# Transposes first in VectorE's turn, mirror loads ahead of the check's, and a second late Q product: one reordering of a Fourier and linear attention kernel

## The chip, the cores and the metric

The kernel runs on one core of a Trainium2 chip. Its engines are TensorE (PE in the profile; its weight loads are PEld), VectorE (DVE), ScalarE (ACT), GpSimd (POOL) and SyncE (SP), which here does nothing but issue DMA transfers. The metric is the time of one execution on the device in microseconds (us), the median of several runs.

## The reference

Two rounds of two blocks on x of 2048 rows and 640 columns, in float32:

```python
x = x + fourier(layernorm(x), dft_seq, dft_hid)
x = x + attention(layernorm(x), wqkv, wo)
x = x + fourier(layernorm(x), dft_seq, dft_hid)
x = x + attention(layernorm(x), wqkv, wo)

def fourier(x, re, im):                  # real part of a 2-D DFT
    a, b = x @ hid_re.T, x @ hid_im.T
    return seq_re @ a - seq_im @ b

def attention(x, wqkv, wo):              # 32 heads of 20 columns
    q, k, v = heads(x @ wqkv)
    pq, pk = phi(q), phi(k)              # t + 1 for t > 0, else exp(t); + 1e-6
    kv, z = pk.T @ v, pk.sum(rows)
    return rows((pq @ kv) / (pq @ z + 1e-6)) @ wo
```

The Fourier matrices are inputs. The kernel uses their symmetries, and checks on the chip that the inputs have them; that check is a part of what VectorE does.

## The kernel before

**Tiles.** The 2048 rows are 16 tiles of 128 rows by 640 columns. A float32 product is made from three products of rounded halves: each operand is split into a hi part (a cast on ScalarE, L125) and a lo part (a subtraction, L126, on VectorE or GpSimd), and hi x hi, hi x lo and lo x hi are added. So one tile's product with a 640 x 640 weight is 30 matrix products of 320 columns (L177).

**A turn.** The attention block's `keys_values` (L282 on) runs two loops, over tiles 0 to 9 and 10 to 15 (`CUT` is 10). Turn n makes K of tile n (30 products), phi of it (three passes on ScalarE, L302 to L304, and one on VectorE, L305), adds it to the sum of K over the rows on GpSimd (L325), and makes Q of tile n and its phi. K and Q need tile n normalized, transposed, and split in hi and lo, and that was made in turn n-1. After each loop `gram` multiplies the tiles with their phi(K), which gives, once V's weight is applied in `combine`, what the reference calls kv. `total` (L390) adds five products with the sum of K.

**Two ways to transpose.** Tiles 1 to 3 are transposed on TensorE (L131). For tiles 4 to 15 (`TURNED`) the normalized tile (L119) is stored to memory (`turn_out`, L139), loaded again in another arrangement (`turn_in`, L144, the "mirror" load), and transposed in 32 x 32 blocks by VectorE (`turned`, L149). `LEADS` (3, 2): turn n normalizes and stores tile n+3, loads tile n+2, and transposes and splits tile n+1.

**The check.** `Check` holds pieces of the Fourier matrices to be compared. `fetch` (L1099) loads up to four tiles of some 346 KB (`ck`), `step` (L1107 to L1124) compares them on VectorE: one reduction, then five custom two-input operations. `STEPS` says after which turns and grams a step is given out; before the change a step ends with the fetch of the next. `SAVES` says when parts of the weights are stored for layer 1, two stores of 320 KB each.

**Order.** SP issues its transfers in the order in which the program is written. The instructions of the other engines are placed by a scheduler, which follows the order of writing unless the table `AHEAD` gives a piece of work an earlier or later place; a step's own operations stay in order among themselves. A late query (`keep`, 1 in both layers) is a Q product that is not made in its turn but at the start of `combine`, where it covers work on other engines. In `combine` the kv products (L432) are followed by a mask (VectorE and GpSimd, from L442) and a hi and lo split, before products with the output weight, 120 rows at a time.

Of the kernel before, what the change touches and what calls it, by code (L numbers as in the profile page):

```python
# [30 lines left out]
STEPS = ((1, 2, 4, 5, 6, 7, 10, 11, 12), (1, 6, 8, 9, 12))  # L31
SAVES = ((4, 5, 8, 13, 15), (1, 4, 8, 10, 11))
# [16 lines left out]
AHEAD = {'2keep00': -60, '2out10': -600, '1q13': 60, '2keep01': 600, '2keep02': 5, '2out02': -20, '1q14': 60, '2out01': 20, '0m1': 60, '0kv5': 200, '1weigh15': -20, '1res13': 5, '2out12': -200, '2weigh1': 5, '2first': 60, '2out13': -200, '0lo10': -200, '0lo03': -600, '0lo02': 20, '0key1': -60, '0key10': 200, '0stats6': -5, '0w0': 200, '0lo13': -60, '0out02': 600, '0pks8': -5, '0stats2': 600, '0hi11': 200, '0lo11': 60, '0normed3': 600, '0out00': -600, '0out11': 5, '0chunks3': 5, '0pks0': 200, '0keep10': 60, '0keep02': 20, '0out03': 600, '0key4': -60, '0chunks4': 20, '0lo12': -60, '0chunks7': -5, '0gram7': -600, '0gram6': -200, '0chunks5': -60, '0chunks13': 60, '0wo0': -20, '0chunks15': -5, '0normed0': -60, '0gram15': 200, '0norm2': 200, '0query15': 5, '0pks2': -60, '0wo5': 5, '0gram2': 200, '0gram8': 5, '0normed4': 5, '0key12': -5, '0stats3': -20, '0stats0': -600, '0query6': 200, '0norm12': 200, '0gram9': -20, '0gram1': 60, '0norm15': -20, '0chunks8': 200, '0weigh1': 60, '0stats8': -200, '0hi00': -5, '0hi13': 5, '0m2': 200, '0query13': 600, '0norm8': -60, '0norm13': 600, '0gram13': -60, '0norm5': -200, '0gram5': -60, '0pks9': -60, '0norm11': -200, '0stats1': 20, '0keep00': 600, '0gram10': -200, '0normed8': 600, '0pks5': 5, '0m5': 20, '0norm7': -600, '0key6': 600, '0query1': 20, '0query2': -60, '0stats7': 60, '0norm0': -5, '0key14': 5, '0weigh0': 20, '0m0': -600, '0query14': -60, '0normed9': 60, '0key8': -5, '0pks10': -600, '0chunks0': 600, '0pz0': -200, '0query12': -5, '0stats12': 20, '0query4': 600, '0zb': -600, '0stats5': 20, '0query10': 200, '2hi12': -600, '3res10': -200, '2pz6': 60, '2norm14': 200, '2kv5': -5, '2pks1': 60, '2hi02': 600, '3q13': -5, '2weigh13': 600, '2norm5': 5, '3q11': 600, '2stats1': -60, '3q5': -200, '2key3': -20, '3weigh11': -20, '2pz4': -20, '3weigh1': -600, '3res9': -20, '2begin': -20, '2hi00': -600, '2stats6': -200, '2stats7': 5, '2chunks1': -20, '2norm2': -600, '3q7': -600, '2kv3': -200, '3res2': 200, '2wo4': -5, '2query6': -600, '2normed8': -600, '2pks0': 20, '2normed6': -60, '2lo02': -60, '2key9': -20, '2chunks9': 20, '2keep10': -20, '2gram11': 200, '2weigh11': -60, '2chunks2': 60, '2pz0': -60, '2m2': -200, '2stats14': 600, '3res13': 600, '2stats10': 200, '3q2': 600, '2key10': 60, '0kv3': -60, '0wo4': 5, '0stats4': 60, '0wo3': -200, '0norm4': -5, '0wo2': -20, '0query7': -600, '0pks1': 200, '0norm10': 60, '0key5': -60, '0normed6': -60, '0pks11': 200, '0pks3': 200, '0pks7': 200, '0normed1': 20, '0chunks9': -20, '0normed13': 20, '0chunks6': 600, '0out12': -60, '0norm1': -20, '0m3': -5, '0stats10': -20, '0normed7': -5, '0key11': 200, '0key9': 60, '0begin': 600, '0lo01': 600, '0gram4': 5, '0query3': -200, '0normed15': -60, '0hi10': -200, '0kv1': 5, '0key0': -200, '0key7': -5, '0chunks2': -60, '0out13': -200, '0chunks11': -600, '0norm6': 5, '0stats14': 60, '0pks14': 20, '0kv0': -200, '0stats13': 5}  # L49


class K:
# [59 lines left out]
    def norm(self, x, out, stats):  # L112
        m, rs, act = stats
        if act == "neg":
            self.nc.vector.tensor_scalar(out, x, m, rs, op0=ALU.add, op1=ALU.mult)
        elif act:
            self.nc.scalar.activation(out, x, AF.Identity, bias=m, scale=rs)
        else:
            self.nc.vector.tensor_scalar(out, x, m, rs, op0=ALU.subtract, op1=ALU.mult)  # L119
# [22 lines left out]
    def turn_in(self, src):  # L142
        z = self.temp()
        self.nc.sync.dma_start(z, src.rearrange("a (j t) c -> (a j) (t c)", t=4))  # L144
        return z

    def turned(self, z, pool):
        t = self.temp()
# [3 lines left out]
        return self.split_chunks(t, pool)  # L152

    def split_chunks(self, tp, pool=0):
        hi, lo = self.temp(F32R), self.temp(F32R)
        self.split(tp[:, :D], hi, lo, pool)
# [25 lines left out]
class Attention:  # L182
    def __init__(self, k, X, order, order2, wqkv, wo, mask, saved=None):
# [3 lines left out]
        self.turns, self.tlows = (TURNED[k.layer], TLOWS[k.layer]) if saved is not None else ((), ())  # L187
# [35 lines left out]
    def normed(self, n):  # L223
# [6 lines left out]
        with self.k.ahead("norm", n):  # L230
            if n in self.turns:
                self.k.norm(x, xn, self.kept[n])
# [841 lines left out]
class Check:  # L1074
# [28 lines left out]
    def step(self, more):  # L1103
# [25 lines left out]
        if more:  # L1129
            self.fetch()  # L1130
# [292 lines left out]
```

## Time and profile before

| | |
|---|---|
| median of 3 runs | 770.46 us (768.66 to 771.43) |
| the profiled execution's own time | 769.41 us |
| its span in the profile | 767.6 us, granted clock 0.997 in the mean |
| PE busy | 736.0 us (96%) |
| VectorE busy | 628.5 us (82%) |
| ScalarE, GpSimd busy | 341.8 us (45%), 261.7 us (34%) |
| DMA | 94.88 MB, mean 124 GB/s |

Where the work lies, in us from the start of the span: the first Fourier block to about 78, layer 0's turns with a first loop that ends at 174, its grams to 219, the second loop to 268, grams to 297, the combine to 315, outputs and the second Fourier block to about 446, layer 1's turns to 539, grams to 583, the second loop to 635, grams to 663, the combine to 682, and the outputs to the end.

An engine's busy time says little about what bounds the kernel where stages differ. The view of waits lists, for an engine, who it waited for, how long in total, how often and the longest; the view by windows gives busy time, granted clock and DMA share of each stretch; the chain of waits goes back from the last instruction and names at each step what was waited for. In all of them a name such as `t<-x,kept` says which tiles are written and read.

### The profile page before, as it was taken

How to read it: one execution, taken by the hardware profiler on the slowest of the kernel's cores; microseconds unless marked ns; L12 is line 12 of the kernel's file. 1: busy time of each engine (PE TensorE's matmuls, PEld its weight loads, DVE VectorE, ACT ScalarE, POOL GpSimd, SP SyncE). 2: the span in 40 equal slices, each digit the busy share in tenths (PEclk: the TensorE clock that was granted, in tenths of full speed). 3: DMA queues.
4: the chain of work that ended last, by engine and by line, in shares of the span. 5: the costliest groups of instructions: out<-in, count | busy, mean ns of one | idle time of the engine just before them, and what ended most of it. 6: DMA issues, size and time to landing. Idle time of an engine off the chain costs nothing.

```text
span 767.6 us, 12773 instructions
## 1 busy us (share of the span) xinstructions
PE 736.0 (96%) x4764; PEld 694.4 (90%) x4764; DVE 628.5 (82%) x1176; ACT 341.8 (45%) x642; POOL 261.7 (34%) x267
## 2 busy tenths in 40 slices
PE   4999999989999999999999999999999999999997
PEld 1388999989999999899977999999999899989996
DVE  7998988978689795988974897899868977599982
ACT  8745445454334553455682334545433445331110
POOL 5248922241012211467762694222101211243300
PEclk9999999999999999999999999999999999999999
DMA  9322346873276741400052223477316615001112
GB/s 332 100 76 89 107 149 190 258 235 110 65 250 201 246 146 26 154 3 2 11 195 70 69 100 118 147 217 234 87 43 215 189 46 151 22 12 68 71 70 73
DMA packets 51231, 94.88 MB, mean 124 GB/s; under 512 B 5044, under 2 KB 19127, under 8 KB 51159
## 3 DMA queue, kind: packets, MB, share of 16 engines
q1 hardware_dynamic: 51159, 93.96, 38.9%
q8 instruction: 40, 0.66, 0.4%
q14 instruction: 32, 0.26, 0.1%
HBM read 73.87 MB, written 19.66 MB: 122 GB/s over the span
## 4 chain that ended last, share of the span: by engine, by line
PE 51%; DVE 28%; ACT 8%; issue 6%; POOL 3%; DMA 3%; SPq 0%; DVEq 0%; POOLq 0%; ACTq 0%
PE ps L177 24%; PE ps L270 16%; DVE junk L1124 6%; PE ps L1049 4%; PE ps L995 3%; DVE t L126 3%; DVE t L149 2%; DVE t L119 2%; DVE w L126 2%; ACT t L125 2%; PE ps L131 1%; PE ps L954 1%; DVE pq L305 1%; DMA ck<-in_ck 1%; DVE st L99 1%
## 5 line engine op out<-in xcount | busy, mean ns | idle before, releaser
L177 PE MATMUL ps<-w,t 128*128 128x320 f32 x2880 | 438.9, 311 | 8.8 <-ACT t L125 5.8
L177 PEld LDWEIGHTS ps<-w,t 128*128 128x128 f32 x2880 | 424.1, 189 | 14.5 <-ACT t L125 10.1
L325 POOL TENSOR_TENSOR t<-t,s 128x640 f32<-128x640 f32 x32 | 64.6, 2018 | 284.7 <-DVE s L305 284.7
L270 PE MATMUL ps<-t,t 128*128 128x256 f32 (+1 forms) x640 | 139.9, 309 | 0.0
L270 PEld LDWEIGHTS ps<-t,t 128*128 128x128 f32 x640 | 106.8, 188 | 0.0
L1124 DVE CUSTOM_DVE_ANT_0 junk<-ck,ck 128x688 bf16<-128x688 f32 (+5 forms) x138 | 99.1, 718 | 4.7 <-DMA ck<-in_ck 1.8
L302 ACT ACTIVATE t<-ps 128x640 f32<-128x640 f32 x64 | 45.1, 705 | 125.1 <-PE ps L177 119.5
L270 PE MATMUL ps<-w,t 128*128 128x384 f32 (+1 forms) x320 | 98.9, 311 | 0.6 <-DVE w L126 0.6
L478 POOL TENSOR_TENSOR t<-pq,t 128x640 f32<-128x640 f32 x32 | 53.3, 1672 | 96.3 <-ACT t L401 46.6
L126 DVE TENSOR_TENSOR t<-t,t 128x640 fp32r<-128x640 f32 x56 | 50.2, 896 | 26.9 <-PE ps L270 16.1
L125 ACT CAST t<-t 128x640 fp32r<-128x640 f32 x56 | 40.8, 728 | 53.6 <-DVE t L119 26.5
L125 ACT CAST t<-ps 128x640 fp32r<-128x640 f32 (+1 forms) x42 | 28.9, 691 | 78.9 <-PE ps L131 77.9
L119 DVE TENSOR_SCALAR t<-x,kept 128x640 f32<-128x640 f32 x60 | 62.7, 1050 | 0.6 <-DMA turn<-t 0.6
L270 PEld LDWEIGHTS ps<-w,t 128*128 128x128 f32 x320 | 60.2, 188 | 1.6 <-DVE w L126 1.5
L995 PE MATMUL ps<-t,u 128*128 128x322 f32 x306 | 48.5, 316 | 1.4 <-ACT t L1022 0.7
L995 PEld LDWEIGHTS ps<-t,u 128*128 128x128 f32 x306 | 46.0, 190 | 2.8 <-ACT t L1022 0.9
L304 ACT ACTIVATE t<-t 128x640 f32<-128x640 f32 x64 | 47.4, 741 | 0.0
L126 DVE TENSOR_TENSOR t<-ps,t 128x640 fp32r<-128x640 f32 (+1 forms) x42 | 34.1, 815 | 5.8 <-ACT t L125 4.8
L305 DVE SCALAR_TENSOR_TENSOR pq<-t,pq 128x640 f32<-128x640 f32 x32 | 27.2, 852 | 13.3 <-ACT t L304 13.3
L149 DVE STREAM_TRANSPOSE t<-t 128x640 f32<-128x640 f32 x24 | 32.1, 1339 | 6.0 <-DMA t<-turn 6.0
L1049 PE MATMUL ps<-cw,ab 128*128 128x512 f32 x80 | 35.4, 596 | 1.6 <-ACT ab L819 0.9
L125 ACT CAST t<-s 128x640 fp32r<-128x640 f32 x32 | 23.2, 725 | 29.4 <-PE ps L270 29.4
(181 smaller groups left out, 905.7 us busy)
## 6 DMA issues: line engine op xcount, KB each, us to landing
ck<-in_ck SPq DMA_DIRECT2D x48, 346.0 KB
ck<-in_ck SPq DMA_DIRECT2D x48, 344.0 KB
turn<-t SPq DMA_DIRECT2D x24, 320.0 KB
t<-turn SPq DMA_DIRECT2D x24, 320.0 KB
save<-w SPq DMA_DIRECT2D x20, 320.0 KB
w<-save SPq DMA_DIRECT2D x20, 320.0 KB
x<-in_x SPq DMA_DIRECT2D x16, 320.0 KB
out<-x SPq DMA_DIRECT2D x15, 320.0 KB
```

Source lines behind the costliest of these rows:

```text
L119: self.nc.vector.tensor_scalar(out, x, m, rs, op0=ALU.subtract, op1=ALU.mult)
L125: self.nc.scalar.copy(hi, src)
L126: self.engine(pool).tensor_tensor(lo, src, hi.bitcast(F32), op=ALU.subtract)
L149: self.nc.vector.transpose(t.rearrange("p (b j t) -> p t b j", b=ND, t=4), z.rearrange("p (t b i) -> p t b i", t=4, b=ND))
L177: nc.tensor.matmul(pu[:m, 512 * h : 512 * h + HD], s, w[:, HD * h : HD * h + HD], start=first, stop=last)
L270: nc.tensor.matmul(self.place(G, c, part), x[:, 128 * c : 128 * c + 128], p[:, f : f + n], start=start and i == 0, stop=stop and i == 2, s ...
L304: nc.scalar.activation(e, e, AF.Exp, scale=-1.0)
L325: nc.gpsimd.tensor_tensor(pksum, pksum, pk, op=ALU.add)
L478: k.nc.gpsimd.tensor_tensor(t1, self.PQ[self.order2[n]], self.zb, op=ALU.mult)
L995: self.k.nc.tensor.matmul(po[:, o : o + 322], s[:, f : f + 128], w[:, x, :], start=start, stop=stop)
L1049: self.k.nc.tensor.matmul(self.sum(j), T.out["o", q][:, 128 * j : 128 * j + 128], self.C[2, g], start=n == 0, stop=n == 3)
L1124: i = nc.vector.tensor_tensor_reduce(k.junk[:, : a.shape[1]], b, a, 1.0, 0.0, op0, op1, o)
```

## The change

1. **Order of a turn.** For a turned tile, the parts of turn n are now written in the order `tfkq`: transpose and split of tile n+1 first, then the feed (norm and store of tile n+3, mirror load of n+2, and the check's fetch), then K, then Q. Before it was feed, K, transpose, Q. Other tiles keep the old order.
2. **The check.** `step` no longer fetches; the fetch stands behind the mirror load in the feed, and in the gram loop. Steps and saves move to other turns (`STEPS`, `SAVES`).
3. **Who does what.** Tile 7 of layer 1 is transposed on TensorE. In layer 0 the lo parts of tiles 7 and 15 are made on GpSimd (`TLOWS`; tile 3 is named too, but is not a turned tile). The norms of tile 2 in layer 0 and of 3 and 5 in layer 1 go to ScalarE (`ANORM`), statistics of more tiles too (`ASTATS`). Eight of the sums of K go from GpSimd to VectorE (`PKSUMS`). Mirror loads of tiles up to 13 take their buffer from Q's pool (`EARLY`).
4. **Late queries.** Layer 0 keeps two (`KEEP`): the first stays at the head of `combine`, the second comes after the kv products. The products of `total` come after the gram of tile 14 in layer 0 and 12 in layer 1, not 10 (`TOTAL`).
5. **Priorities.** Entries of `AHEAD` are changed, removed and added.

```diff
-STEPS = ((1, 2, 4, 5, 6, 7, 10, 11, 12), (1, 6, 8, 9, 12))
-SAVES = ((4, 5, 8, 13, 15), (1, 4, 8, 10, 11))
+STEPS = ((1, 2, 3, 4, 5, 6, 10, 11, 12), (2, 4, 8, 9, 12))
+SAVES = ((4, 5, 8, 10, 13), (0, 6, 7, 11, 12))
...
-TURNED = (tuple(range(4, 16)), tuple(range(4, 16)))
-TLOWS = ((), ())
+TURNED = ((4, 5, 6, 7, 8, 9, 10, 11, 12, 13, 14, 15), (4, 5, 6, 8, 9, 10, 11, 12, 13, 14, 15))
+TLOWS = ((3, 7, 15), ())
 LEADS = (3, 2)
+ORDERS = ('tfkq', 'tfkq')
+ANORM = ((2,), (3, 5))
+KEEP = (2, 1)
+TOTAL = (4, 2)
+EARLY = (14, 13)
+PKSUMS = ((1, 7, 13, 14), (2, 6, 11, 12))
...
-ASTATS = ((11,), (1,))
-VSTATS = ((4, 6, 8, 9, 10, 11, 13), ())
+ASTATS = ((4, 10, 11, 13, 14), (1, 4, 10, 15))
+VSTATS = ((0, 3, 4, 7, 8, 11, 13, 15), (1, 11, 13, 15))
...
-    def norm(self, x, out, stats):
+    def norm(self, x, out, stats, on_act=False):
         m, rs, act = stats
-        if act == "neg":
+        if on_act:
+            nb = self.small([128, 1], "nb")
+            self.nc.gpsimd.tensor_tensor(nb, m, rs, op=ALU.mult)
+            if act != "neg":
+                self.nc.gpsimd.tensor_scalar(nb, nb, -1.0, None, op0=ALU.mult)
+            self.nc.scalar.activation(out, x, AF.Identity, bias=nb, scale=rs)
+        elif act == "neg":
...
+                turns = n + 1 in self.turns
+                for what in ORDERS[k.layer] if turns else "fkcq":
+                    if what == "f":
+                        feed()
+                        if check is not None and check.more:
+                            check.fetch()
+                    elif what == "t":
+                        turn()
+                    elif what == "k":
+                        key()
+                        pks.append(pk)
+                    elif what == "c":
+                        if n and n + 1 < NT:
+                            chunks()
+                    elif n < NT - keep:
+                        query(mid=chunks if not turns and n + 1 < NT and not n else None)
+                    else:
+                        late.append(query)
...
+                if check is not None and check.more:
+                    check.fetch()
                 self.gram(G + [tail], ready, n == a, n == b - 1, a == 0)
...
-                if n == CUT:
+                if n == CUT + TOTAL[k.layer]:
                     self.total(G, pksum)
...
-        self.now = None
-        if more:
-            self.fetch()
+        self.now, self.more = None, more
```

VectorE in turn 4 of layer 0, before. `t_1377` is the transposed tile 5, L305 are phi of K (`s`) and of Q (`pq`), L119 the norm of tile 8, and L1107 and L1124 the check step (`ca`, `junk`, `cm`; the short read of the result after each piece is left out here and below).

```order
L149 STREAM_TRANSPOSE t_1377<-t_1242 128x4x160
L305 SCALAR_TENSOR_TENSOR s_1339<-t_1371,s_1339 128x640
L126 TENSOR_TENSOR t_1380<-t_1377,t_1379 128x640
L119 TENSOR_SCALAR t_1436<-x_96,kept_1437 128x640
L305 SCALAR_TENSOR_TENSOR pq_1383<-t_1415,pq_1383 128x640
L1107 TENSOR_REDUCE ca<-ck_1222 128x1
L1124 ISA junk,cm<-ck_1224,ck_1222 128x692
L1124 ISA junk,cm<-ck_1226,ck_1224 128x692
L1124 ISA junk,cm<-ck_1228,ck_1226 128x692
L1124 ISA junk,cm<-ck_1222,ck_1228 128x519
L1124 ISA junk,cm<-ck_1222,ck_1228 128x173
L149 STREAM_TRANSPOSE t_1488<-t_1337 128x4x160
```

And with the change (L161 is the transpose, L138 the lo part, L131 the norm, L321 phi, L1140 and L1157 the step):

```order
L161 STREAM_TRANSPOSE t_1333<-z_1242 128x4x160
L1157 ISA junk,cm<-ck_1125,ck_1131 128x173
L321 SCALAR_TENSOR_TENSOR pq_1289<-t_1321,pq_1289 128x640
L1140 TENSOR_REDUCE ca<-ck_1244 128x1
L1157 ISA junk,cm<-ck_1246,ck_1244 128x692
L138 TENSOR_TENSOR t_1335<-t_1333,t_1334 128x640
L131 TENSOR_SCALAR t_1339<-x_128,kept_1340 128x640
L1157 ISA junk,cm<-ck_1248,ck_1246 128x692
L1157 ISA junk,cm<-ck_1250,ck_1248 128x692
L321 SCALAR_TENSOR_TENSOR s_1332<-t_1392,s_1332 128x640
L1157 ISA junk,cm<-ck_1244,ck_1250 128x519
L161 STREAM_TRANSPOSE t_1444<-z_1351 128x4x160
```

The transpose moved ahead of the phi of the query of the turn before, the lo part and the norm now stand ahead of phi of K, and the step is spread through the turn instead of standing in one piece between phi of Q and the next transpose.

SP's queue around the same turns, before (`ck` are the check's tiles, `turn` the stores, `t` the mirror loads, `save` the weights' stores):

```order
L1099 DMA ck_1222<-in_ck 128x692
...
L1099 DMA ck_1228<-in_ck 128x692
L139 DMA turn_1240<-t_1230 128x4x160
L144 DMA t_1242<-turn_1127 128x640
L139 DMA turn_1335<-t_1325 128x4x160
L144 DMA t_1337<-turn_1240 128x640
L221 DMA save_468<-w_675 128x640
L221 DMA save_469<-w_676 128x640
L1099 DMA ck_1428<-in_ck 128x692
```

And with the change (two of the four check loads of a fetch are left out of both):

```order
L1132 DMA ck_1244<-in_ck 128x692
...
L1132 DMA ck_1250<-in_ck 128x692
L151 DMA turn_1349<-t_1339 128x4x160
L156 DMA z_1351<-turn_1240 128x640
L1132 DMA ck_1353<-in_ck 128x692
...
L1132 DMA ck_1359<-in_ck 128x692
L237 DMA save_468<-w_675 128x640
L237 DMA save_469<-w_676 128x640
```

The check's loads now stand directly behind the store and the mirror load of the same turn; before, they were issued with the end of the step before, which gave two turns' stores and loads without a fetch between.

TensorE in the combine of layer 0, before: the end of the kv products (L432), then the products with the output weight (`w_3343`, `w_3374`).

```order
L432 MATMUL ps_3352<-s_2424,s_3243 120x120
L432 MATMUL ps_3352<-s_2425,s_3245 120x120
L177 MATMUL ps_3393<-w_3279,w_3343 40x320 x2
L177 MATMUL ps_3393<-w_3280,w_3343 40x320 x2
...
L131 MATMUL ps_3404<-ident,t_3283 128x128 x5
L177 MATMUL ps_3421<-w_3249,w_3374 120x320 x2
```

And with the change:

```order
L465 MATMUL ps_3310<-s_2415,s_3201 120x120
L465 MATMUL ps_3310<-s_2416,s_3203 120x120
L193 MATMUL ps_3352<-w_715,t_2843 128x320 x2
L193 MATMUL ps_3352<-w_716,t_2843 128x320 x2
...
L193 MATMUL ps_3352<-w_739,t_2844 128x320 x2
L193 MATMUL ps_3388<-w_3237,w_3301 40x320 x2
```

Between the kv products and the first product with the output weight there now stand the 30 products of the second late query (`ps_3352`), of which three rows are shown.

More of the change, by code (lines that the diff above doesn't have):

```diff
@@ L186, in __init__ @@
         self.kept = {}
-        self.turns, self.tlows = (TURNED[k.layer], TLOWS[k.layer]) if saved is not None else ((), ())
+        self.turns, self.tlows, self.anorm = (TURNED[k.layer], TLOWS[k.layer], ANORM[k.layer]) if saved is not None else ((), (), ())
     def wt(self):
@@ new lines, in feed @@
+                def feed(n=n):
+                    for m in range(n + 1, n + 1 + lead) if n == 0 else (n + 1, n + lead):
+                        if m < NT and m not in out and (m == n + 1 or m in self.turns):
+                            with k.ahead("normed", m):
+                                out[m] = self.normed(m)
+                    for m in range(n + 1, n + 1 + fetch) if n == 0 else (n + fetch,):
+                        if m < NT and m in self.turns:
+                            out[m] = k.turn_in(out[m], m < EARLY[k.layer])
@@ L1086, in fetch @@
     def fetch(self):
-        k, self.now, free = self.k, [], 4
+        k, self.now, self.more, free = self.k, [], False, 4
         while self.pieces:
```

70 lines of the change are left out of this document (29 added, 41 removed).

## The prediction

> **What bounds the kernel now.** I read the page's busy times first, then the waits of TensorE, then busy time by stage, then the chain of waits.
>
> ```profile
> PE 736.0 (96%) x4764; PEld 694.4 (90%) x4764; DVE 628.5 (82%) x1176; ACT 341.8 (45%) x642; POOL 261.7 (34%) x267
> ...
> PE ps L672 <- DMA x<-in_x: 10.6, 1, 10.6
> PE ps L177 <- ACT t L125: 5.8, 9, 1.8
> PE ps L177 <- DVE t L126: 3.0, 6, 0.8
> ...
> PE ps L390 <- POOL t L325: 0.4, 1, 0.4
> ```
>
> TensorE (PE) works for 736.0 of 767.6 us; only its 31.6 us of idle time, and work done at a lowered clock, can be won. One third, 10.6, is the first load and is not touched. The next two rows are products of the turn loops (L177) waiting for the hi part (L125) or the lo part (L126) of the next tile: 8.8 us. They are the change's target. What each stage loses, by windows over the four turn loops and the combine of layer 0 (columns: span of the window, PE busy, PEld, VectorE = DVE, ScalarE = ACT, GpSimd = POOL, granted clock, DMA share, GB/s):
>
> ```profile
> 106.22:174.33 68.11, 64.60 (x423) 63.01 (x421) 57.76 (x102) 34.36 (x55) 20.48 (x16) 0.97 0.74 232
> 218.78:268.28 49.50, 49.10 (x333) 48.39 (x332) 40.46 (x69) 24.50 (x39) 10.88 (x5) 1.00 0.69 224
> ...
> 474.69:538.99 64.30, 62.89 (x423) 61.58 (x421) 57.25 (x96) 32.84 (x51) 15.25 (x8) 1.00 0.66 201
> ...
> 583.31:635.00 51.69, 49.13 (x333) 48.34 (x331) 43.95 (x86) 24.07 (x38) 9.95 (x5) 1.00 0.44 137
> ...
> 583.47 8.81 PE ps L177 x60
> ```
>
> The last row, from the chain of waits, is an undisturbed turn: 60 products in 8.81 us, 30 for K and 30 for Q. The first window holds turns 3 to 9 of layer 0: 68.11 - 7 x 8.81 = **6.44** lost. The second, turns 10 to 15 with one late query (5.5 turns): 49.50 - 48.46 = **1.04**. Layer 1 the same: 64.30 - 61.67 = **2.63** and 51.69 - 48.46 = **3.23**. Together 13.34 us.
>
> Why they are lost is seen on VectorE, in a turn with a check step (a timeline; start, duration):
>
> ```profile
> 131.09 1.34 DVE L149 STREAM_TRANSPOSE t<-t 128x640 f32<-128x640 f32 x1
> 132.28 0.81 DVE L305 SCALAR_TENSOR_TENSOR s<-t,s 128x640 f32<-128x640 f32 x1
> 133.22 0.83 DVE L126 TENSOR_TENSOR t<-t,t 128x640 fp32r<-128x640 f32 x1
> 133.97 1.90 DVE L119 TENSOR_SCALAR t<-x,kept 128x640 f32<-128x640 f32 x1
> ...
> 136.52 0.32 DVE L1107 TENSOR_REDUCE ca<-ck 128x1 f32<-128x173 f32 x1
> 136.76 0.86 DVE L1124 CUSTOM_DVE_ANT_0 junk<-ck,ck 128x692 bf16<-128x692 f32 x1
> ...
> 140.26 0.34 DVE L1124 CUSTOM_DVE_ANT_0 junk<-ck,ck 128x173 bf16<-128x173 f32 x1
> ...
> 140.52 1.35 DVE L149 STREAM_TRANSPOSE t<-t 128x640 f32<-128x640 f32 x1
> ...
> 133.23 2.29 POOL L325 TENSOR_TENSOR t<-t,s 128x640 f32<-128x640 f32 x1 [7.71 <-DVE s L305]
> ...
> L119 DVE TENSOR_SCALAR t<-x,kept x60: 586/610/1896, 65.3 to 648.0; 128x640 f32<-128x640 f32 x60
> ```
>
> From one transpose to the next VectorE needs 9.43 us and is never idle; TensorE would need 8.81. So each such turn lets TensorE overtake by 0.62 us, and the transpose of the tile that TensorE wants next stands *behind* the whole check step, 4.0 us from 136.52 to 140.52. Part of the 9.43 is a collision: the normalization took 1.90 us beside GpSimd's K sum (133.23 to 135.52), and its median is 0.61.
>
> The Trainium skill, "SBUF — State Buffer", section "Who interferes with whom", says that VectorE and GpSimd share a port pair as an exclusive lock, which whoever starts first holds for its whole instruction; this trace agrees (1.90 beside the sum, 0.61 alone). By that rule the check's two-input operations could be blocked as well wherever the new order puts them beside the sum; by it a check turn would cost VectorE up to 9.5 us instead of the 8.4 that I use below (8.14 + 1.38, an estimate), which the slack found below would still pay over five turns, so the sum stays.
>
> The price of such a turn shows where the slack is used up, at turns 8 and 9:
>
> ```profile
> 162.95 1.44 PE L177 MATMUL ps<-w,t 128*128 128x320 f32 x8 [1.77 <-ACT t L125]
> 165.19 9.30 PE L177 MATMUL ps<-w,t 128*128 128x320 f32 x52 [0.81 <-DVE t L126]
> 162.93 2.21 DVE L126 TENSOR_TENSOR t<-t,t 128x640 fp32r<-128x640 f32 x1
> 162.87 1.58 POOL L325 TENSOR_TENSOR t<-t,s 128x640 f32<-128x640 f32 x1 [2.67 <-DVE s L305]
> ...
> 165.19:167.00 1.81, 1.81 (x7) 1.81 (x8) 1.75 (x3) 1.30 (x2) 0.00 (x0) 0.50 1.08 382
> ```
>
> Two waits of 1.77 and 0.81 us, then a granted clock of 0.50: 52 products took 9.30 us where 52/60 of 8.81 is 7.64, so 1.66 us of the 6.44 is clock. It goes when the stalls go.
>
> **The change: the turn first.** No product is removed; PE's work is the same but for five transposes (below). VectorE now does transpose, the last check piece, phi of the query, reduce, one check piece, lo part, norm, then the rest of the check. When is the next lo part ready? The old query's phi needs ScalarE first:
>
> ```profile
> 124.38 0.71 ACT t L302
> 125.09 0.06 ACT pq L303
> 125.15 0.42 issue
> 125.57 0.75 ACT t L304
> ```
>
> That is 1.94 us after the query's last product. Then 0.81 (phi) + 0.32 (reduce) + 0.86 (a check piece) + 0.83 (lo) make 4.76; I say 5.1 with gaps. It is needed at 8.81: **3.7 us of slack**, where today there is none. Wherever that slack is not used, TensorE never waits. VectorE's work in a check turn falls to 9.43 - 1.29 = 8.14 if the norm no longer meets the sum. The sum then starts beside the last check pieces and the transpose; a two-input operation could be stretched by 0 to 1.38 (2.21 - 0.83, the lo part at 162.93), and as the 1.34 transpose covers most of the sum's 1.58, I take 0.3: 8.44, below 8.81. So VectorE alone stalls nothing.
>
> **The ring through DMA.** The norm of tile n+3 now waits for the lo part of tile n+1; its store is issued before the mirror load of n+2 on SP's queue, and the next turn's transpose waits for that load. Ring: transpose 1.34, check piece 0.34, phi 0.81, reduce 0.32, piece 0.86, lo 0.83, norm 0.61 (5.11), SP's store, and the load.
>
> ```profile
> 111.19 2.85 SPq L1099 DMA_DIRECT2D ck<-in_ck  x4
> 114.09 0.43 SPq L139 DMA_DIRECT2D turn<-t  x1
> 114.62 0.45 SPq L144 DMA_DIRECT2D t<-turn  x1
> 120.54 1.35 DVE L149 STREAM_TRANSPOSE t<-t 128x640 f32<-128x640 f32 x1 [1.94 <-DMA t<-turn]
> ...
> 214.20 7.82 SPq L1099 DMA_DIRECT2D ck<-in_ck  x5
> 217.69 0.33 DVE L1107 TENSOR_REDUCE ca<-ck 128x1 f32<-128x172 f32 x1 [1.01 <-DMA ck<-in_ck]
> ```
>
> With four check loads and a store ahead of it the mirror load took 120.54 - 114.62 = 5.9 us; a check load with the queue empty took 217.69 - 214.20 = 3.5. The ring is 5.11 + 0.43 + (3.5 to 5.9) = 9.0 to 11.4 us, that is e = 0.2 to 2.6 us over 8.81 for every check turn in a row (without a step, 1.5 us falls out and it holds). Behind the store on SP's queue now stand also the check's own loads: issued when the norm is done, some 5.7 us into the turn, they land 3.5 to 5.9 later, at 9.2 to 11.6, and VectorE asks for the first at 8.81 + 1.94 + 0.81 = 11.6: covered, with nothing to spare at the upper end. In the new order the checks come after the mirror loads, but the store still runs beside; I take the middle, 4.7, so e = 1.4. Check turns in which a turned tile hangs on it: 3 to 6 (four) and 10 to 12 (three) in layer 0; 3 to 5 and 10 to 12 in layer 1, since tile 7 is now turned on PE. Each row of turns starts with 3.7 us of slack. What stays lost: 4e - 3.7 = 1.9; 3e - 3.7 = 0.5; 0.5; 0.5.
>
> **Smaller parts.**
>
> ```profile
> L126 POOL TENSOR_TENSOR w<-raw,w 128x640 fp32r<-128x640 f32 x4 | 7.1, 1775 | 3.2 <-ACT w L125 3.2
> 308.27 0.77 PE L131 MATMUL ps<-ident,t 128*128 128x128 f32 x5
> 308.79 2.72 PE L177 MATMUL ps<-w,w 120*120 120x320 f32 x16
> 312.50 0.56 PE L177 MATMUL ps<-w,w 120*120 120x320 f32 x2 [0.99 <-DVE w L126]
> 313.43 2.02 PE L177 MATMUL ps<-w,w 120*120 120x320 f32 x12 [0.37 <-DVE t L126]
> ```
>
> Layer 0's turn 14 is now only 30 products (4.4 us), and tile 15's lo is made on GpSimd (1.78 us for 0.83), so its K product may wait 0 to 1.6 us; if VectorE comes to that transpose after the check piece and the sum it now makes itself, the lo is about 0.4 late: I take **0.5**. Five transposes in layer 1: next products start 308.79 - 308.27 = **0.5** later. The late query (4.4 us of products) after the kv products covers the combine's mask and lo parts: the waits of 0.99 + 0.37 = **1.4** go. The total after four (two) grams instead of none finds its sum ready: **0.4** (L390 above). Norms and statistics on ScalarE, at 45%, and sums on VectorE in turns without much else: nothing, hidden under products; without that cover, 0.8 us a piece. The checks' fetches in the gram loop: nothing, VectorE has the room there.
>
> Sum of what goes: 6.44 - 1.9 = 4.5; 1.04 - 0.5 - 0.5 = 0.0; 2.63 - 0.5 - 0.5 = 1.6; 3.23 - 0.5 = 2.7; 1.4; 0.4: **10.6 us**. The profiled execution's span is 767.6 and its own time 769.41; the median of the runs, 770.46, is 1.05 above it. So a span of 757.0, a time of 758.8, and a median of **759.9**.
>
> **Rivals.** Stalls after the change are 13e - 14.8 + 1.0 (13 check turns, four slacks, the two small losses), against 15.1 now (13.34 + 1.4 + 0.4).
>
> *All stalls go.* If the load takes 3.5 us as from an empty queue, the slack is never used up: 15.1 - 0.5 = 14.6 go, **755.9**. For it: the load now stands ahead of the checks. Against: DMA share 0.74 in that window.
>
> The Trainium skill, "DMA: Bandwidth & Descriptors", section "Anatomy of one DMA — SWDGE (gpsimd) path", gives 2.0 us plus bytes at 436 GB/s, about 2.75 us for 320 KB (an estimate from that page, for another kind of queue). By it this rival is the result; the 5.9 us above disagrees, the 3.5 is nearer.
>
> *Half comes back.* The load takes 5.1 us: e = 1.85, stalls 10.3, gain 4.8, **765.7**. For it: six steps in a row with saves (two 320 KB stores each) at turns 4 and 5.
>
> *The order does not reach the stalls*: a tile's transpose, though first, is as late as now because its load is. Only 1.8 (combine and total) goes: **768.7**.
>
> *Slower: the ring takes VectorE's place.* The load keeps its 5.9 us: e = 2.6, stalls 13 x 2.6 - 13.8 = 20.0, 4.9 more than now: **775.4**. It decides from e = 2.2, a load of 5.5 us. For it: the one mirror load that the waits show took 5.9. Against: the four check loads that stood in front of it now stand behind. A norm stretched to 1.90 inside the ring does the same at a load of 4.2.
>
> **How the numbers follow.** The forecast 0.48, all gone 0.16, half 0.17, not reached 0.07, slower 0.12. Range for 8 in 10: from 755.5 (all gone) to 768.0, leaving out most of the last two. About 0.3%, 2.3 us, can be told from no change. Faster by more: the first three and a little of "not reached", 0.82; within: the rest of it, 0.06; slower 0.12.
>
> **What would show it.** Right: in turns 3 to 9 of layer 0 TensorE's windows near 63 us, no wait of 1.8, no clock of 0.50; norms at 0.61 in check turns; combine 0 without the 0.99. Wrong: VectorE's transposes waiting for the mirror load by more than 1 us in every check turn (then the ring rules, and each further us of load costs 13), norms still at 1.9, or new waits at tiles 7, 8 and 15.

## The result and the profile after

The changed kernel takes **759.07 us** in the median (758.40 to 760.75, 4 runs), beside 769.88 us before on the same chips: a ratio of 0.9862, 95% interval 0.9836 to 0.9888. Forecast were 759.9, between 755.5 and 768.0. The profiled execution (759.65 us) has a span of 757.7 us, before 767.6.

The page and TensorE's (PE's) waits of the changed kernel, the counterparts of the first lines shown of before (L193 is the line of the products, L286 of the grams, L143 of PE's transposes):

```profile
PE 732.2 (97%) x4769; PEld 695.1 (92%) x4769; DVE 597.0 (79%) x1162; ACT 356.0 (47%) x673; POOL 245.2 (32%) x262
...
PE ps L286 <- DVE w L138: 2.6, 3, 1.1
PE ps L143 <- DVE t L537: 2.2, 1, 2.2
PE ps L193 <- DVE t L138: 1.2, 2, 1.0
```

The 8.8 us in which products waited for a hi or lo part are down to 1.2, none of it in the turn loops. (Of the 8.8, 7.4 lay in the four loop windows of the prediction; the rest lay in the combine and in other blocks.) But two rows that were 0.6 us each before now stand above it: the grams wait for lo parts, 2.6 us, and a transpose of the outputs waits for L537, 2.2 us. The windows say where (turns 3 to 9 of layer 0, its first grams, its second loop, its second grams, the combine; then turns 3 to 9 and the second loop of layer 1):

```profile
106.30:168.22 61.92, 61.92 (x423) 61.60 (x421) 48.91 (x92) 34.21 (x57) 14.88 (x12) 1.00 0.68 222
168.22:214.61 46.39, 44.72 (x303) 43.97 (x301) 38.71 (x75) 20.03 (x32) 2.37 (x2) 1.00 0.49 144
214.61:258.77 44.16, 44.16 (x303) 43.97 (x301) 33.63 (x67) 23.40 (x38) 9.34 (x7) 1.00 0.74 238
258.77:287.60 28.83, 27.72 (x192) 27.40 (x191) 17.75 (x31) 11.50 (x21) 2.09 (x1) 1.00 0.34 111
287.60:310.04 22.44, 21.43 (x163) 20.16 (x162) 18.80 (x39) 12.17 (x24) 9.88 (x6) 1.00 0.09 23
469.51:531.68 62.17, 62.17 (x428) 62.16 (x427) 53.66 (x110) 34.40 (x55) 15.22 (x14) 1.00 0.61 189
...
575.82:624.23 48.41, 48.41 (x332) 48.41 (x331) 36.96 (x85) 25.00 (x41) 5.92 (x4) 1.00 0.43 145
```

In all four loops PE is busy for the whole window: 61.92 us for seven turns of 8.81 (61.67). Where the 9.9 us of span went, block by block, each from the first product or gram of the block to that of the next one (a late query, 30 products or 4.41 us, moved from the second loop of layer 0 to its combine and is put back here):

| block | before | after | saved |
|---|---|---|---|
| layer 0: first loop (turns 0 to 9) | 96.23 | 90.07 | 6.16 |
| first grams | 44.45 | 46.39 | -1.94 |
| second loop | 49.49 | 44.16 + 4.41 | 0.92 |
| second grams | 28.28 | 28.83 | -0.55 |
| combine, outputs, second Fourier block | 149.50 | 153.88 - 4.41 | 0.03 |
| layer 1: first loop | 92.94 | 90.20 | 2.74 |
| first grams | 44.32 | 44.14 | 0.18 |
| second loop | 51.69 | 48.41 | 3.28 |
| second grams | 28.15 | 27.51 | 0.64 |
| combine and outputs | 104.47 | 105.98 | -1.51 |

The loops gave 13.1 us; some 3.2 of it were given back elsewhere. The table compares one execution of each kernel; what e6 says below of the last row shows that such rows can hold more than a kernel's own cost.

### The profile page after: what moved, and what is told of

Same layout as the page of the kernel before. It is cut to its first block, busy times and chain, and to the rows that moved or that the text cites. A ratio compares the mean times of both kernels' runs of the same rounds, so it can differ in the third digit from the quotient of the medians.

```text
span 757.7 us, 12763 instructions
## 1 busy us (share of the span) xinstructions
PE 732.2 (97%) x4769; PEld 695.1 (92%) x4769; DVE 597.0 (79%) x1162; ACT 356.0 (47%) x673; POOL 245.2 (32%) x262
## 4 chain that ended last, share of the span: by engine, by line
PE 71%; DVE 13%; DMA 5%; ACT 4%; POOL 2%; issue 2%; SPq 1%; DVEq 0%; ACTq 0%
PE ps L193 41%; PE ps L286 18%; PE ps L1028 4%; PE ps L1082 3%; DMA z<-turn 3%; PE ps L143 2%; PE ps L465 2%; DVE t L138 2%; PE ps L987 1%; DMA ck<-in_ck 1%; DVE t L531 1%; DVE ps L527 1%; DMA x<-in_x 1%; DVE x L553 1%; DVE junk L1157 1%
## 5 line engine op out<-in xcount | busy, mean ns | idle before, releaser
L193 PE MATMUL ps<-w,t 128*128 128x320 f32 x2880 | 435.7, 311 | 0.7 <-DVE w L138 0.3
L193 PEld LDWEIGHTS ps<-w,t 128*128 128x128 f32 x2880 | 424.2, 188 | 2.6 <-DVE t L138 0.6
L286 PE MATMUL ps<-t,t 128*128 128x256 f32 (+1 forms) x640 | 140.0, 309 | 0.2 <-ACT t L137 0.2
L1157 DVE CUSTOM_DVE_ANT_0 junk<-ck,ck 128x688 bf16<-128x688 f32 (+5 forms) x138 | 103.8, 752 | 7.9 <-DMA ck<-in_ck 6.2
L286 PEld LDWEIGHTS ps<-t,t 128*128 128x128 f32 x640 | 107.2, 188 | 0.4 <-ACT t L137 0.4
L353 POOL TENSOR_TENSOR t<-t,s 128x640 f32<-128x640 f32 x24 | 43.4, 1808 | 181.7 <-DVE s L321 174.7
L286 PE MATMUL ps<-w,t 128*128 128x384 f32 (+1 forms) x320 | 98.8, 310 | 2.6 <-DVE w L138 2.6
L318 ACT ACTIVATE t<-ps 128x640 f32<-128x640 f32 x64 | 45.1, 705 | 106.5 <-PE ps L193 106.1
L286 PEld LDWEIGHTS ps<-w,t 128*128 128x128 f32 x320 | 60.1, 188 | 3.7 <-DVE w L138 3.7
L138 DVE TENSOR_TENSOR t<-t,t 128x640 fp32r<-128x640 f32 x53 | 45.9, 865 | 20.7 <-ACT t L137 19.5
L138 DVE TENSOR_TENSOR t<-ps,t 128x640 fp32r<-128x640 f32 (+1 forms) x43 | 35.0, 816 | 8.7 <-ACT t L137 8.7
L321 DVE SCALAR_TENSOR_TENSOR pq<-t,pq 128x640 f32<-128x640 f32 x32 | 28.2, 881 | 14.3 <-ACT t L320 14.3
L112 POOL TENSOR_TENSOR kept<-ve,mhalf 128x1 f32<-128x1 f32 x32 | 21.1, 675 | 54.3 <-DVE ve L111 53.7
L321 DVE SCALAR_TENSOR_TENSOR s<-t,s 128x640 f32<-128x640 f32 x32 | 26.6, 832 | 9.9 <-ACT t L320 9.9
L1082 PEld LDWEIGHTS ps<-cw,ab 128*128 128x128 f32 x80 | 14.8, 190 | 21.0 <-issue 18.6
```

The source lines that it names most:

```text
L138: self.engine(pool).tensor_tensor(lo, src, hi.bitcast(F32), op=ALU.subtract)
L193: nc.tensor.matmul(pu[:m, 512 * h : 512 * h + HD], s, w[:, HD * h : HD * h + HD], start=first, stop=last)
L286: nc.tensor.matmul(self.place(G, c, part), x[:, 128 * c : 128 * c + 128], p[:, f : f + n], start=start and i == 0, stop=stop and i == 2, s ...
L318: nc.scalar.activation(h2(e), halves(pu), AF.Relu, scale=-1.0)
L321: nc.vector.scalar_tensor_tensor(out, e, 1e-6, out, op0=ALU.add, op1=ALU.add)
L353: k.engine(n not in PKSUMS[k.layer]).tensor_tensor(pksum, pksum, pk, op=ALU.add)
```

## The experiments

All times are medians, with the kernel before in the same runs (768.8 to 769.0 us in each set of e1 to e12; the changed kernel's own set had 769.88 for before, so small differences to it go by the ratios). Blocks of the profiles, as in the table above (us; in the second loop and the combine of kernels with two late queries the 4.41 us are not put back):

| kernel | time | loop | grams | loop | grams | combine to Fourier | loop | grams | loop | grams | rest |
|---|---|---|---|---|---|---|---|---|---|---|---|
| before | 768.9 | 96.2 | 44.5 | 49.5 | 28.3 | 149.5 | 92.9 | 44.3 | 51.7 | 28.2 | 104.5 |
| changed | 759.1 | 90.1 | 46.4 | 44.2 | 28.8 | 153.9 | 90.2 | 44.1 | 48.4 | 27.5 | 106.0 |
| e1 old order | 780.7 | 91.8 | 44.5 | 57.3 | 29.1 | 153.7 | 96.6 | 44.4 | 50.8 | 27.6 | 104.5 |
| e2 old fetch | 816.3 | 104.8 | 47.9 | 63.0 | 29.2 | 153.6 | 99.2 | 45.2 | 59.3 | 28.3 | 104.5 |
| e3 order alone | 854.9 | 117.5 | 50.9 | 67.8 | 28.4 | 150.9 | 115.7 | 51.2 | 59.5 | 28.3 | 104.3 |
| e4 fetch alone | 768.7 | 93.6 | 44.4 | 50.6 | 28.2 | 149.4 | 93.7 | 44.4 | 51.7 | 28.9 | 104.5 |
| e5 order and fetch | 758.2 | 89.8 | 48.0 | 48.4 | 28.3 | 149.4 | 89.9 | 44.8 | 48.5 | 28.2 | 104.3 |
| e9 tables alone | 804.9 | 103.3 | 44.4 | 58.9 | 29.0 | 153.7 | 107.1 | 44.5 | 52.0 | 27.6 | 106.1 |

### e1 to e5 and e9: which part does it

The change has three parts that can be taken apart: the order of a turn, the place of the check's fetch, and all the rest (tables, late queries, totals, priorities). The edits:

```diff
 e1: the order set back
-ORDERS = ('tfkq', 'tfkq')
+ORDERS = ('fktq', 'fktq')
 e2: the fetch set back (in step)
-        self.now, self.more = None, more
+        self.now, self.more = None, False
+        if more:
+            self.fetch()
 e5: before's STEPS, SAVES, TURNED, TLOWS, ASTATS, VSTATS, AHEAD, and
+ANORM = ((), ())
+KEEP = (1, 1)
+TOTAL = (0, 0)
+EARLY = (0, 0)
+PKSUMS = ((), ())
 e3: e5 with the edit of e2
 e4: e5 with the edit of e1
 e9: the changed kernel with the edits of e1 and e2
```

e1, order set back:

> The changed kernel with the order of writing in a turned turn set back (feed and fetch, K, transpose, Q); all other edits stay. Theory (the order took the stalls of the four turn loops away): they come back, turns 3 to 9 of layer 0 take 66 us or more (61.9 in the changed kernel, 68.1 before), and the time is 767 to 773 us. Rival (the tables did it: who makes norms, lo parts, sums, and where steps and saves lie): 759 to 762, loops as in the changed kernel.

Measured 780.67 us (ratio to before 1.0150, 1.0126 to 1.0173): slower than either theory said, and not where the theory put it. The first loop of layer 0 is 1.7 us longer than in the changed kernel, not 4; the second 13.1. VectorE of e1 there:

```profile
240.91 0.87 DVE L1157 CUSTOM_DVE_ANT_0 junk<-ck,ck 128x688 bf16<-128x688 f32 x1 [2.51 <-DMA ck<-in_ck]
241.71 1.30 DVE L161 STREAM_TRANSPOSE t<-z 128x640 f32<-128x640 f32 x1
...
251.10 0.88 DVE L1157 CUSTOM_DVE_ANT_0 junk<-ck,ck 128x688 bf16<-128x688 f32 x1 [1.55 <-DMA ck<-in_ck]
251.90 1.35 DVE L161 STREAM_TRANSPOSE t<-t 128x640 f32<-128x640 f32 x1
```

With the fetch behind the mirror load, the check's tiles arrive late, and with the old order the transpose stands behind the check piece that waits for them (2.51, 1.55 us; 11.7 us of such waits over the run, 3.9 in e4, which has before's tables). Of the 13.1 us, 7.1 are waits of PE, and 6.1 are products at a lowered clock (granted 0.50 from 244.3 to 251.1 and from 264.8 to 271.6).

e2, fetch set back:

> The changed kernel with the check's fetch set back to the end of a step, so that four check loads stand ahead of the store and the mirror load on SP's queue. Theory (the ring through DMA has little room): the mirror load takes about 6 us in each check turn, turns 3 to 9 of layer 0 take 65 to 68 us, the time is 764 to 768. Rival (the fetch's place costs nothing, only VectorE's order counts): 759 to 760.5.

Measured 816.28 us (1.0610, 1.0581 to 1.0640): the theory's direction, and 48 us beyond its range. VectorE's transposes wait 56.1 us for mirror loads, 11.5 in the changed kernel.

e3, the order alone:

> Before's numbers for all tables, priorities, late queries and totals, and before's fetch at a step's end; only the order of a turned turn is the new one. Theory: most of the 13 us of loop stalls goes by the order alone, the time is 760 to 764. Rival (order without the fetch's new place gives a ring through DMA as slow as the stalls it takes away): 767 to 776.

Measured 854.88 us (1.1120, 1.1100 to 1.1140): the rival's mechanism, far beyond its price. VectorE and SP's queue of e3 in one turn:

```profile
139.84 0.60 DVE L131 TENSOR_SCALAR t<-x,kept 128x640 f32<-128x640 f32 x1
...
142.94 0.34 DVE L1157 CUSTOM_DVE_ANT_0 junk<-ck,ck 128x173 bf16<-128x173 f32 x1
...
150.90 1.31 DVE L161 STREAM_TRANSPOSE t<-t 128x640 f32<-128x640 f32 x1 [6.88 <-DMA t<-turn]
...
141.26 2.85 SPq L1132 DMA_DIRECT2D ck<-in_ck  x4
144.16 0.43 SPq L151 DMA_DIRECT2D turn<-t  x1
144.69 0.45 SPq L156 DMA_DIRECT2D t<-turn  x1
...
SPq L1132 <- DVE cn L1157: 172.7, 18, 16.6
DVE t L161 <- DMA t<-turn: 132.6, 21, 7.8
```

This is the ring closed through SP. The norm is done at 140.44, but its store goes out at 144.16: ahead of it on SP stand the four check loads of the next step, and they wait until VectorE's check pieces (to 143.3) have freed their buffers; over the run SP waits 172.7 us for such pieces, 18 times. (In the kernel before it waits 132.0 us in the same way; there the transposes wait only 6.0 us for mirror loads, here 132.6.) The mirror load follows at 144.69 and, behind those four loads in the DMA engines, is used at 150.90: 6.2 us. So the whole check step and 6.2 us of load are in the ring; the transposes of this stretch start at 134.26 and 150.90, 16.6 us apart where PE needs 8.81. The loss is not waits alone: of the 83.6 us by which the span is longer than before's, 56.4 are idle time of PE, and 27.2 are work that takes longer (PE is busy 763.2 us, not 736.0; the mean granted clock is 0.956, not 0.997).

e4, the fetch alone:

> Before's numbers for all tables and before's order of a turn; only the check's fetch stands behind the mirror load and in the gram loop. Theory: no effect while the transpose stands behind the whole check step, 769 to 772. Rival (the mirror loads' lateness was the stall all along): 765 or less.

Measured 768.73 us; 0.9995 (0.9985 to 1.0004): no effect, as the theory said.

e5, order and fetch together, everything else as before:

> Before's numbers for all tables, priorities, late queries and totals, with both the new order of a turn and the fetch behind the mirror load. Theory A (order and fetch only work as a pair: the order puts the store and the mirror load into the path, the fetch's place keeps the check's loads and their wait for free buffers out of it): most of the loop stalls go, 760 to 764 us. Theory B (the ring also needs the tables: mirror loads in Q's buffers, norms and sums elsewhere, other steps): the ring stays above 8.8 us a turn, 770 or more.

Measured **758.24 us**; 0.9863 (0.9838 to 0.9888), the same as the whole change (0.9862). Theory A holds, theory B falls. The ring in e5, VectorE's transposes and SP's loads:

```profile
122.43 1.35 DVE L161 STREAM_TRANSPOSE t<-t 128x640 f32<-128x640 f32 x1 [1.02 <-DMA t<-turn]
132.30 1.35 DVE L161 STREAM_TRANSPOSE t<-t 128x640 f32<-128x640 f32 x1 [0.73 <-DMA t<-turn]
141.06 1.36 DVE L161 STREAM_TRANSPOSE t<-t 128x640 f32<-128x640 f32 x1 [0.61 <-DMA t<-turn]
149.94 1.36 DVE L161 STREAM_TRANSPOSE t<-t 128x640 f32<-128x640 f32 x1 [0.71 <-DMA t<-turn]
...
118.78 0.45 SPq L156 DMA_DIRECT2D t<-turn  x1
128.69 0.37 SPq L156 DMA_DIRECT2D t<-turn  x1
137.49 0.45 SPq L156 DMA_DIRECT2D t<-turn  x1
146.35 0.38 SPq L156 DMA_DIRECT2D t<-turn  x1
```

From issue to use a mirror load takes 3.6 us each time (122.43 - 118.78 to 149.94 - 146.35), and the transposes come 9.9, 8.8 and 8.9 us after the one before: VectorE still waits for each load, 0.6 to 1.0 us, but in the last two turns the ring keeps PE's pace.

e9, the tables alone:

> The changed kernel with both the order of a turn and the fetch's place set back: tables, late queries, totals and priorities alone. Theory (the pair of order and fetch is the whole gain, and the rest was chosen to fit it): no faster than before, 769 to 785 us. Rival (the tables are worth something by themselves, and the pair would have gained more without its losses): 762 to 768.

Measured 804.85 us; 1.0460 (1.0442 to 1.0478). The theory's sign, 20 us beyond its range. The tables are worth nothing by themselves and cost 36 us where the pair is missing. Check pieces wait 16.4 us for their tiles and transposes 11.8 us for mirror loads (1.8 and 6.0 before); which of the tables does this was not tested. Taken together, in us:

| | neither | order | fetch | both |
|---|---|---|---|---|
| before's tables | 768.9 | 854.9 | 768.7 | 758.2 |
| the change's tables | 804.9 | 816.3 | 780.7 | 759.1 |

The gain is an interaction: with before's tables 11 us for the pair, nothing for the fetch, a loss of 86 for the order.

### e6: the mirror loads' buffers

```diff
-EARLY = (14, 13)
+EARLY = (0, 0)
```

> The changed kernel with all mirror loads back in the pool of temporary buffers. Theory A: no effect, 758 to 760. Theory B (a mirror load waits on SP's queue until a temporary buffer is free, with the check's loads behind it): the loads are issued later, VectorE's transposes wait for them, 765 or more.

Measured **755.79 us** (755.64 to 756.03); 0.9834 (0.9812 to 0.9855). Both theories missed: it is faster than the change by 3.3 us (2.2 by the ratios to before), and the ranges of the runs do not touch (758.40 to 760.75). It is also 2.4 us faster than e5 of the same set, whose range (757.09 to 759.17) it does not touch either: so once the pair is there, the tables without this one are worth something. The loops are the same (89.7, 44.0, 90.2, 48.4); the first grams take 45.0 instead of 46.4 and the rest 103.4 instead of 106.0. The rest first, in the two profiles (of the changed kernel, then of e6; VectorE, then GpSimd):

```profile
673.48 1.85 DVE L531 TENSOR_TENSOR t<-pq,rden 128x600 f32<-128x600 f32 x1
675.25 1.52 DVE L537 TENSOR_TENSOR t<-pq,rden 128x40 f32<-128x40 f32 x1
...
673.12 3.60 POOL L511 TENSOR_TENSOR t<-pq,t 128x640 f32<-128x640 f32 x2 [5.89 <-DVE den L528]
...
676.92 1.05 PE L143 MATMUL ps<-ident,t 128*128 128x128 f32 x5 [2.20 <-DVE t L537]
...
676.90:683.40 6.50, 6.48 (x35) 6.50 (x36) 5.04 (x15) 0.69 (x1) 0.00 (x0) 0.74 0.14 53
```

```profile
672.55 0.71 DVE L531 TENSOR_TENSOR t<-pq,rden 128x600 f32<-128x600 f32 x1
673.19 1.54 DVE L537 TENSOR_TENSOR t<-pq,rden 128x40 f32<-128x40 f32 x1
...
672.50 4.24 POOL L511 TENSOR_TENSOR t<-pq,t 128x640 f32<-128x640 f32 x2 [6.21 <-DVE cktop L1179]
...
674.87 0.74 PE L143 MATMUL ps<-ident,t 128*128 128x128 f32 x5 [0.83 <-DVE t L537]
```

VectorE's rows stand in the same order there. In the changed kernel GpSimd's first multiplication was released by `den` (L528), began at 673.12 and took 1.57 of the 3.60 us, and VectorE's L531, 0.36 us later, took 1.85. In e6 it was released by a later operation, `cktop` (L1179), the two began within 0.05 us of each other, L531 took 0.71, and the multiplication took 2.17 of the 4.24 us. So one of the two pays, and PE's next transpose hangs on VectorE: it waits 2.20 instead of 0.83 us. This goes with the edit: the six kernels with `EARLY` as in the change (the changed one, e1, e2, e7, e8, e9) have a wait of 2.0 to 2.2 us there, and e6 and e10 to e12 one of 0.8 to 0.9. Why the mirror loads' buffers change what GpSimd waits for was not followed.

The other part does not go with the edit. After the wait the changed kernel's profile has a granted clock of 0.50 for 3.4 us (the 0.74 is the mean of 6.5 us), which costs some 1.7 us. Behind the same wait e9 has it too, but e1, e2, e7 and e8 have a clock of 1.00, and their last blocks take 104.4 to 104.7 us, not 106.0. It differs between executions of one kernel, too: the two fastest of the changed kernel, 758.40 and 758.49 us, have a mean clock of 0.999, and 3.4 us at 0.50 alone would lower the mean by 0.002. Why the first grams gain 1.4 us was not taken apart further; they take 45.5 and 45.6 us in e8 and e7, which keep the changed kernel's buffers, and 45.3 to 45.8 in e10 to e12, which have e6's.

### e7 and e8: sums of K, and the second late query

```diff
 e7
-PKSUMS = ((1, 7, 13, 14), (2, 6, 11, 12))
+PKSUMS = ((), ())
 e8
-KEEP = (2, 1)
+KEEP = (1, 1)
```

> The changed kernel with all sums of K on GpSimd again. Theory (the new order alone keeps the norm out of the sum's way): norms stay at 0.6 us, 758 to 760.5. Rival (the collision moves to the check's pieces, the lo parts and the gram's norms and is paid there): 761 to 765.

Measured 759.54 us (758.78 to 760.17); 0.9886 (0.9864 to 0.9908). As the theory said: 4 of 61 norms take over 1.5 us with all sums on GpSimd, 2 in the changed kernel, and 20 of 60 before, and the time does not tell this kernel from the changed one.

> The changed kernel with one late query in layer 0 instead of two. Theory (the second one covers part of the combine; the stage tables of the two profiles give 0.7 us): 759.3 to 761. Rival (its phi on VectorE stands ahead of the lo parts that the rows wait for, and gives as much back): 758 to 759.2.

Measured 758.10 us (756.88 to 758.52); 0.9866 (0.9844 to 0.9888): in the rival's range, and the same as the changed kernel's by the ratios. e11 below looks for the reason.

### e10 to e12: what is left

All three start from e6.

```diff
 e10: turn 9
...
-                for what in ORDERS[k.layer] if turns else "fkcq":
+                for what in ("kqgtf" if n == CUT - 1 else ORDERS[k.layer]) if turns else "fkcq":
...
+                    elif what == "g":
+                        with k.ahead("gram", 1):
+                            second = self.gram_ready(1, pks[1])
...
 e11: combine
...
-        for q in late[1:]:
-            q()
+        after = [q(hold=True) for q in late[1:]]
...
         rest = rows(NE - 1)
+        for f in after:
+            f()
 e12: e11, and
+PKSUMS = ((1, 7, 13, 14, 15), (2, 6, 11, 12, 15))
```

> The changed kernel with all mirror loads in the temporary pool (755.8 us), and in turn 9 the transpose of tile 10 and the norm of tile 12 written behind the operands of the second gram. Theory (TensorE waits in the first grams of layer 0 because VectorE does work first that is not needed until the grams are over): the first gram block falls from 45.0 to 44.4 to 44.6 us, the time by 0.3 to 0.6, 755.2 to 755.5. Rival (VectorE is simply late after the loop, whatever the order): no change, 755.8.

Measured 757.16 us (756.89 to 757.78): the theory falls. The first grams take 45.8 us in both layers (45.0 and 44.7 in e6): the transpose and the norm that were put off now stand in front of later lo parts, and the wait at 174.08 of 0.61 us became two:

```profile
173.37 0.44 PE L286 MATMUL ps<-w,t 128*128 128x384 f32 x1 [0.41 <-DVE w L138]
178.81 0.44 PE L286 MATMUL ps<-w,t 128*128 128x384 f32 x1 [0.80 <-DVE w L138]
```

> The changed kernel with all mirror loads in the temporary pool (755.8 us), and phi of the second late query written behind the first rows of the output product in the combine. Theory (that phi, 1.6 us on VectorE, stands ahead of the lo part that the rows wait for; TensorE waits 1.0 us for it): the wait goes, 754.7 to 755.2. Rival (VectorE has as much to do in any order, so the wait moves to a later product): 755.5 to 756.

Measured 755.69 us (755.19 to 756.43), against 755.79 of e6. The wait did go; the combine of e6, then of e11:

```profile
305.80 2.91 PE L193 MATMUL ps<-w,w 120*120 120x320 f32 x18 [1.04 <-DVE t L138]
```

```profile
303.37 5.02 PE L193 MATMUL ps<-w,w 120*120 120x320 f32 x30
308.65 0.74 PE L143 MATMUL ps<-ident,t 128*128 128x128 f32 x5 [0.27 <-DVE w L138]
```

The thirty products with the output weight now run through, and the blocks from the combine to the Fourier block take 153.15 instead of 153.78 us; the time is the same within its runs. So the second late query hides the mask and the lo parts, and its own phi then stood in the way, for some 0.6 us. That this is why e8 found it worth nothing is not shown, since taking phi out of the way did not make the time shorter.

> The kernel of e11 (755.7 us) with the sum of K of tile 15 moved from GpSimd to VectorE in both layers. Theory (TensorE's wait of 1.1 us in the second gram block of layer 0 is a norm that takes 1.74 us for 0.61 beside that sum on GpSimd): the norm takes 0.6, the wait falls to 0.3 or less, the second gram blocks fall from 28.9 and 27.6 to about 28.2 and 27.5, the time to 754.6 to 755.2. Rival (the sum costs VectorE its 0.8 us in the same place): the wait stays at 0.8 to 1.1, 755.4 to 756.

Measured **755.31 us** (754.78 to 755.49); 0.9821 (0.9805 to 0.9837), the best of all. Between the two: the norm fell to 0.61 us, but the sum that VectorE now makes stands ahead of it, and of PE's 1.1 us wait 0.56 is left:

```profile
260.85 0.82 DVE L353 TENSOR_TENSOR t<-t,s 128x640 f32<-128x640 f32 x1
261.58 0.61 DVE L131 TENSOR_SCALAR t<-x,kept 128x640 f32<-128x640 f32 x1
...
262.98 0.39 PE L286 MATMUL ps<-w,t 128*128 128x256 f32 x1 [0.56 <-DVE w L138]
```

The second grams take 28.4 instead of 28.9 us. Against e11 alone (755.69) the gain is within what the runs can tell.

## Why the prediction came out right, and where it was wrong

**What bounds, and where the time is to be won:** right. PE's waits for hi and lo parts in the loops were the target and went; the clock of 0.50 after the waits went with them (granted clock 1.00 in all four windows).

**The loops: too low.** 4.5 + 0.0 + 1.6 + 2.7 = 8.8 us were forecast to go of 13.3. In the same windows 6.19, 0.93 (49.50 - 44.16 - 4.41), 2.13 and 3.28 went: 12.5, which in the loops is the rival "all stalls go". The step that failed is the price of the ring: 1.9, 0.5, 0.5 and 0.5 us were to stay lost to it, and the windows show 0.2 (turn 8), 0.1, nothing and nothing. The load was put at 4.7 us, halfway between 3.5 and 5.9; e5 measures 3.6 each time. In the changed kernel's first loop two loads take 3.5 and 3.6 us (the transposes at 115.99 and 124.66), but the two after them are later:

```profile
115.99 1.35 DVE L161 STREAM_TRANSPOSE t<-z 128x640 f32<-128x640 f32 x1 [1.04 <-DMA z<-turn]
124.66 1.36 DVE L161 STREAM_TRANSPOSE t<-z 128x640 f32<-128x640 f32 x1 [0.70 <-DMA z<-turn]
134.81 1.36 DVE L161 STREAM_TRANSPOSE t<-z 128x640 f32<-128x640 f32 x1 [1.54 <-DMA z<-turn]
147.14 1.35 DVE L161 STREAM_TRANSPOSE t<-z 128x640 f32<-128x640 f32 x1 [2.18 <-DMA z<-turn]
150.09 0.82 DVE L138 TENSOR_TENSOR t<-t,t 128x640 fp32r<-128x640 f32 x1
...
130.69 0.45 SPq L156 DMA_DIRECT2D z<-turn  x1
137.22 0.91 SPq L237 DMA_DIRECT2D save<-w  x2
140.34 0.52 SPq L156 DMA_DIRECT2D z<-turn  x1
```

The loads issued at 130.69 and 140.34 took 4.1 and 6.8 us to their use. Ahead of each stand two stores of weights (127.08 and 137.22) and, directly before these, the last loads of a fetch; which of them makes the load late was not separated. So here the ring did fall behind: the transposes are 8.7, 10.2 and 12.3 us apart, together 4.7 us over three turns of 8.81, or e = 1.6 a turn, close to the 1.4 that was forecast, and the waits of 1.04, 1.54 and 2.18 us are of the size that was to show the forecast wrong. That it cost PE almost nothing is the second mis-sizing. Four check turns were counted and only three came into it before turn 7, which has no step; and the lo part of tile 8, done at 150.91, was 0.6 us after the start of its turn (150.30), yet PE lost 0.2 there, since the turn's first products read the hi part alone. The slack was 3.7 by the forecast and about 4.5 in effect.

**The price of a load.** The Trainium skill ("DMA: Bandwidth & Descriptors", "Anatomy of one DMA — SWDGE (gpsimd) path"; about 2.75 us for 320 KB, an estimate from that page, for another kind of queue) spoke for the rival in which all stalls go. These runs show 3.6 us from issue to use behind the turn's own store (e5), and 6.2 behind four check loads and a store (e3). The estimate is 0.9 below the first: the time of a load on its own would have been nearer for the loops, and blind to e3.

**VectorE in a check turn:** right. The forecast allowed a two-input operation 0 to 1.38 us more beside one of GpSimd and took 0.3 for a turn. The worst check piece took 2.09 us for 0.87, so 1.22 more, beside GpSimd's lo part of tile 7:

```profile
137.22 2.09 DVE L1157 CUSTOM_DVE_ANT_0 junk<-ck,ck 128x692 bf16<-128x692 f32 x1
...
137.00 1.57 POOL L138 TENSOR_TENSOR t<-t,t 128x640 fp32r<-128x640 f32 x1 [2.29 <-ACT t L137]
```

The Trainium skill ("SBUF — State Buffer", "Who interferes with whom") says that a VectorE instruction with two inputs in SBUF contends with a GpSimd instruction that reads SBUF, and the trace agrees (2.09 us for 0.87). The slack paid for it.

**Tile 15's lo part and turn 14, 0.5 lost:** 0.1; the second loop of layer 0 ran at 44.16 us for 5 turns (44.05) after the 4.41 moved out. **Five transposes, 0.5 lost:** right (62.17 against 61.67).

**The combine, 1.4 gained:** too high. 18.73 became 22.44 - 4.41 = 18.03, so 0.7, and a wait of 1.0 us stayed there; the step forgot that the late query brings its own phi to VectorE ahead of the lo parts (e11), and nothing of it reached the time (e8). **The total, 0.4 gained:** that wait went, but the second grams of layer 0 got another, for the lo part behind a norm of 1.75 us.

**Not foreseen:** losses outside the loops. The first grams of layer 0 lost 1.94. This goes with the new order: every kernel that has it takes 45.0 to 50.9 us there, and every kernel with the old one 44.4 to 44.5. That PE arrives 6 us earlier is not the reason, since in e2 and e3 it arrives later than before and waits there for VectorE all the same (47.9 and 50.9 us); what makes VectorE late was not found (e10 put off two of its operations, and the grams became longer). The last block lost 1.51 in the profiled execution, for the two reasons that e6 shows: the collision with GpSimd, which the forecast did not look for there, and a lowered clock that other executions don't have.

**The number: luck.** In the span 3.7 us more than forecast came from the loops, and 4.4 less from everything else (1.8 forecast, 9.9 - 12.5 = -2.6 measured): the sum came out 0.8 us from the measured median because two errors cancelled. The mechanism, the loops' waits that go once the transpose stands first and its load ahead of the check's, is borne out by e1 to e5; the split of the gain is not.

**The rival "slower: the ring takes VectorE's place"** was real, only not in this kernel: it is e3 and e2, where the transposes wait 132.6 and 56.1 us for mirror loads. The forecast had its mechanism, the check loads ahead of the mirror load, and priced it as a load of 5.9 us, 775 us. It left out that those loads also wait for buffers that VectorE's check frees, which puts the store behind the whole check step.

## What to carry to other kernels

When work is put first on one engine, follow what it depends on through every in-order queue: here a queue with a transfer that waits for a buffer in front of one that is wanted at once turned a gain of 11 us into a loss of 86. Two edits that each do nothing or harm can be the whole gain together, so test the pair as well as each part. And count what the other blocks lose: here 3.2 of the 13.1 us that the loops gave.

## What the runs showed of the hardware that was not expected

When a VectorE operation and one of GpSimd meet, one of the two pays, and a few tenths of a microsecond decide which. The same L531, in the same place of the program, took 1.85 us when GpSimd's multiplication (1.57 us) had begun 0.36 us earlier, and 0.71 us when the multiplication had begun 0.05 us earlier and took 2.17 us itself.

The same wait of TensorE need not have the same price. Behind 2.0 to 2.2 us of waiting in one place of the program the granted clock was 0.50 for 3.4 us in two profiles (the changed kernel and e9) and 1.00 in four (e1, e2, e7 and e8).
